# Layernorm on ScalarE, later transposes, and earlier loads in a fused attention and ReGLU kernel on one core

## The chip, the core and the metric

The kernel runs on one core of one Trainium2 chip. The core has a matrix engine (TensorE, PE in the profile, with its weight loads listed apart as PEld), VectorE (DVE), ScalarE (ACT), GpSimd (POOL), and SyncE (SP), which here only issues DMA transfers. Each engine works through its own instructions in order and waits on semaphores for the others. The metric is the device time of one execution in microseconds, as the median of several runs.

## The reference

`x` has 2048 rows (tokens) of 576 columns, float32.

```python
xn = layernorm(x)                                  # over the 576 columns, eps 1e-5
q, k, v = split(xn @ wqkv)                         # 32 heads of 18 columns
s = softmax(q @ k.T * 18**-0.5) @ v @ wo           # full attention, per head
gate = xn @ W_gate; gate = gate * (gate > 0)       # 576 -> 4608
B = (gate * (xn @ W_up)) @ W_down                  # 4608 -> 576
return x + s * silu(B)
```

## The kernel before

Every float32 operand of a matmul is split into a high and a low part in the matmul's reduced format, and each product is made of three matmuls (high x high, high x low, low x high). `split_full` does this for results in PSUM: ScalarE copies the high part out, VectorE subtracts for the low part. `split_pool` does it for weights: POOL casts, then subtracts.

Matmuls use 64 of the 128 rows of the array, and two of them run at the same time on the two halves: two *lanes*. A planner, the class `Lanes`, writes PE's order out by hand (`keep` fixes program order). `lanes.window(parts, scores, inserts)` issues the parts of the two lanes in turn; `inserts` are calls that are made when a given share of the window has been issued. When a lane must start a bank that the other lane ended, `part` puts a fence on ScalarE or VectorE, and the matmul waits for it.

The first stage goes through four groups `g` of 512 tokens. The rows of group 0 are loaded, their statistics taken (`stats`: bn_stats and bn_aggr on VectorE, then a square root on ScalarE and a refined reciprocal), normalized (`normalized_rows`, into `xn`, with 64 extra columns that repeat the last ones), and turned (`turn`: four PE transposes per chunk of 128 columns into `tps`, five chunks, split into the tile `x`). Then, for each group, one window holds the q and k products (`pq`: four pairs of head blocks with the weights `wqk0` to `wqk3`, and at odd groups `qk_last` with `wqk4`), 216 matmuls of 512 columns, 270 at odd groups. In this window the next group is normalized and turned, by inserts from `rows_to_features`. A second window holds 216 matmuls for v (`pv`, weights `wv`). q, k and v go out to DRAM (`qd`, `kd`, `vd`).

In the last group, the memory of the transposed rows `xB` is given to a pool `at` of key and query tiles (`kT`, `qT`), filled by many small loads on SP (`load_k`, `load_q`); score maxima (`pm`) of the first heads run between the v products.

The long loop follows: `cycle(k)` computes two units of 128 hidden columns each, gate and up products (`pg`, `pu`, with the split weights `gw` of `up_weights`), their product `hh`, the down product (`py`, weights `dw`), and between them the attention of two heads. In `cycle(0)` the order of the two units on the two lanes is "+U +W -U -W". A tail applies `wo` and the last sum.

Of the kernel before, what the change touches and what calls it, by code (L numbers as in the profile page):

```python
# [9 lines left out]
F32 = mybir.dt.float32  # L10
# [18 lines left out]
class Lanes:  # L29
# [4 lines left out]
    def __init__(self, banks, make, matmul, fence):  # L34
        self.make, self.matmul, self.fence = make, matmul, fence
        self.t = [0.0, 0.0]
        self.last = 0.0
        self.free = [0.0] * banks
        self.used = [False] * banks
        self.server = {"V": 0.0, "A": 0.0}  # L40
        self.main = [deque(), deque()]
        self.n = self.synced = self.fences = 0
        self.wrote = [0] * banks
        self.left = []

    def take(self, now):
# [84 lines left out]
        return p.open + self.FENCE <= self.t[lane]  # L131

    def part(self, p):
        by = min("AV", key=lambda e: self.server[e])
        self.fence(by, p.ps)
        self.fences += 1
        p.open = max(self.server[by], p.end + self.FENCE)
        self.server[by] = p.open
# [69 lines left out]
def kernel(  # L208
# [46 lines left out]
    def keep(ins):  # L255
        return tc.keep_in_program_order(ins)
# [37 lines left out]
    def split_pool(hi, lo, raw):  # L294
        keep(nc.gpsimd.tensor_copy(hi, raw))  # L295
        keep(nc.gpsimd.tensor_tensor(lo, raw, hi.bitcast(F32), ALU.subtract))  # L296
# [113 lines left out]
    with ExitStack() as st:  # L410
# [1 line left out]
        xBs = st.enter_context(ExitStack())  # L412
        xB = pool(xBs, "xB", KX + 1, "right")

        def weights(name, n, outs, pl=one, first=False, **kw):
            gw = pl.tile([P, 2, KS, n], F32R, name=name, **kw)
            o = 0
            for cols in outs:
                m = sum(c[2] for c in cols[0])
                rg = one.tile([P, KS, P], F32, tag="rgw", name="rgw", bufs=2)[:, :, :m]  # L420
                load9(rg, cols)
                hi, lo = gw[:, 0, :, o : o + m], gw[:, 1, :, o : o + m]
                if first:
                    nc.scalar.activation(hi, rg, AF.Copy)
                    nc.gpsimd.tensor_tensor(lo, rg, hi.bitcast(F32), ALU.subtract)
                else:
                    split_pool(hi, lo, rg)
                o += m
            return gw

        def load_rows(g):
            xt = one.tile([P, 4, D], F32, name="xt", bufs=2)
            if g == 0:
                for j in range(4):
                    nc.sync.dma_start(xt[:, j], x2[j * P : (j + 1) * P, :])
            else:
                nc.sync.dma_start(xt, rows512(x2, g))
            return xt

        def stats(xt, ln):  # L440

            stat = one.tile([P, 4, 2, 6], F32, name="stat")
            mv = one.tile([P, 4, 2], F32, name="mv")
            for j in range(4):
                for h in range(2):
                    keep(nc.vector.bn_stats(stat[:, j, h, :], xt[:, j, h * HC : (h + 1) * HC]))
                keep(nc.vector.bn_aggr(mv[:, j, :], stat[:, j, :, :]))
                yield
            ve, sd, r0, r1, r2, rs = (
                one.tile([P, 4], F32, name=f"ln{i}") for i in range(6)  # L450
            )
            keep(nc.vector.tensor_scalar(ve, mv[:, :, 1], EPS, None, op0=ALU.add))
            nc.scalar.activation(sd, ve, AF.Sqrt)
            nc.vector.reciprocal(r0, sd)
            nc.vector.tensor_tensor(r1, r0, r0, ALU.mult)
            nc.vector.tensor_tensor(r2, r1, ve, ALU.mult)
            nc.vector.tensor_scalar(r1, r2, -0.5, 1.5, op0=ALU.mult, op1=ALU.add)
            nc.vector.tensor_tensor(rs, r0, r1, ALU.mult)
            ln += [xt, mv, rs]
            yield  # L460

        def normalized_rows(xt, mv, rs, xn):
            for j in range(4):
                nc.vector.tensor_scalar(
                    xn[:, j, :D], xt[:, j], mv[:, j, 0:1], rs[:, j : j + 1], op0=ALU.subtract, op1=ALU.mult
                )
                nc.vector.tensor_scalar(
                    xn[:, j, D:], xt[:, j, C4:], mv[:, j, 0:1], rs[:, j : j + 1], op0=ALU.subtract, op1=ALU.mult
                )
                if j % 2:  # L470
                    yield

        def turn(g, xn, i):

# [49 lines left out]
        def qk_last(gw, g):  # L524
            return pair(
                ("pq", "pq"), (xs[g], xs[g + 1]), lambda rows, s, a, xr: (gw[rows, a, s, :], xr),
                512, [qk_steps(4, g + m, m, True) for m in range(2)],
            )
# [37 lines left out]
        wqk = []  # L566

        def qk_weights(b):
            kw = dict(pl=ws, tag="gw") if b == 3 else {}
            wqk.append(  # L570
                weights(f"wqk{b}", P, [[[(wqkv, b * P, P)], [(wqkv, D + b * P, P)]]], first=b < 2, **kw)
            )

        qk_weights(0)
        qk_weights(1)
        nxt = load_rows(1)
        qk_weights(2)
        qk_weights(3)
        wv = weights(
            "wv", HC, [[[(wqkv, 2 * D + m * VH, VH)], [(wqkv, 2 * D + HC + m * VH, VH)]] for m in range(3)]  # L580
        )
        wqk.append(weights("wqk4", P, [[[(wqkv, C4, DT), (wqkv, D + C4, DT)]] * 2], pl=ws, tag="gw"))
        xn0 = one.tile([P, 4, D + DT], F32, name="xn")
        for _ in normalized_rows(*ln0, xn0):
            pass
        for i in range(KX):
            turn(0, xn0, i)

        def stepped(gen, at_):
            return [(w, lambda: next(gen, None)) for w in at_]  # L590

        for g in range(NQ):
            fill = iter(())
            if g + 1 < NQ:
                fill = rows_to_features(g + 1, nxt)
            pairs = [qk_pair(b, wqk[b], g) for b in range(4)]
            first = pairs[:2] + ([qk_last(wqk[4], g - 1)] if g % 2 else [])
            parts = [a + b for a, b in zip(in_turn(first), in_turn(pairs[2:]))]
            spread = [0.1 + 0.85 * i / 12 for i in range(12)]
            ins = stepped(fill, spread)  # L600
            lanes.window(parts, None, ins)
            if g + 1 < NQ:
                spill(g)
            if g + 2 < NQ:
                nxt = load_rows(g + 2)
            if g == NQ - 1:
                xBs.close()
                at = pool(right, "at", 1, "right")
                for i in range(NRING):
                    kT = at.tile([P, 512], F32R, name=f"kT{i}")  # L610
                    nc.gpsimd.memset(kT.bitcast(F32), 1.0)
                    ring.append(kT)
                load_q(0, 0)
                for c in range(NQ):
                    load_k(0, c)
                load_q(0, 1)
                up_weights(0)
                pms = [maxima(0, h) for h in range(2)]
            vp = v_pairs(wv, g)
            va_, vb_ = in_turn(vp[:2]), in_turn(vp[2:])  # L620
            scores = None
            if g == NQ - 1:
                scores = [(deque(pms[h].popleft() for _ in range(NP)), deque()) for h in range(2)]
            lanes.window([a + b for a, b in zip(va_, vb_)], scores)
            for _ in fill:
                pass

    two = pool(right, "two", 2, "right")
    acc = right.enter_context(ExitStack())
# [241 lines left out]
    def cycle(k, scores):  # L871

        up_weights(k + 1)
        ups = []
        ins = []
        downs = down(k - 1) if k else []
        down_weights(k)
        sums = dict(zip("UWabcd", [up(k), up(k + 1), *downs]))
        if k > N1:
            orders = ("+a +U -a +b -U +W -b +c -W +d -c -d", "+a +U -a -U +b +W -b +c -W +d -c -d")  # L880
        elif k:
            orders = ("+U +a -U +b -a -b +W +c -W +d -c -d",) * 2
        else:
            orders = ("+U +W -U -W",) * 2
        parts = [[sums[o[1]][l ^ (o[0] == "-")] for o in orders[l].split()] for l in range(2)]
        turn_over = units[k + 1][1] == NF - 1 and k + 2 < len(units)
        ins.append((0.55, lambda: (gus.pop(k), up_weights(k + 2))))

        if turn_over:
            ins.append((0.8, lambda: load_x(units[k + 2][0], 0)))  # L890
        lanes.window(parts, scores, ins)
        gus.pop(k + 1)
        down_weights(k + 1)
        if k:
            store_y(k - 1)
        if turn_over:
            del xcur[units[k][0]]
            for c in range(1, KX):
                load_x(units[k + 2][0], c)
# [180 lines left out]
```

## Time and profile before

| | us |
|---|---|
| median of 3 runs | 2640.25 (2640.12 to 2640.27) |
| profiled execution | 2642.54 |
| its span | 2640.5 |
| PE busy in it | 2607.2 |
| DVE, ACT, POOL busy | 1733.0, 1464.0, 1442.1 |
| mean granted TensorE clock | 0.996 |

The profile records one execution. Its span runs from the first to the last recorded instruction; 2.04 us lie around it. In rows of the timeline the first number is the start in us from the beginning of the span, the second the duration, then engine, line, operation, output and inputs with their shapes, the count, and in brackets how long the engine had been idle and what released it. Rows of groups give busy time and the mean of one instruction in ns. A matmul's duration overlaps with the next ones', so the pace of a run of matmuls is read from their starts.

### The profile page before, as it was taken

The page shows a single profiled execution, that of the slowest core. Times are in us where ns is not written, and L with a number is a line of the kernel's source. Part 1 is how long each engine was busy: PE and PEld are TensorE (multiplying, and loading weights), DVE is VectorE, ACT ScalarE, POOL GpSimd, SP SyncE. Part 2 cuts the span into 40 slices and gives each one's busy share as a digit, 9 for nine tenths or more (in the row PEclk, how much of TensorE's full clock was granted, in tenths as well). Part 3 has the DMA queues.
Part 4 walks back from the last instruction along what each step waited for, and adds up shares of the span by engine and source line. Part 5 has one row for each costly group of instructions (what it writes and reads, how often), then busy time and mean ns, then how long its engine had stood idle before and what let it go on. Part 6 is the DMA issues. An engine that isn't in the chain of part 4 may idle for free.

```text
span 2640.5 us, 62759 instructions
## 1 busy us (share of the span) xinstructions
PE 2607.2 (99%) x25436; PEld 2119.1 (80%) x25436; DVE 1733.0 (66%) x2888; ACT 1464.0 (55%) x2755; POOL 1442.1 (55%) x1273
## 2 busy tenths in 40 slices
PE   7998999999999999999999999999999999999999
PEld 5997887778887777777778778887777777778789
DVE  5325557777777777777777777777777777776124
ACT  2221226666666666666666666666666666666662
POOL 5234886555555555555555555555555555555555
PEclk9998999999999999999999999999999999999999
DMA  8644332222232222222242222222233222222247
GB/s 253 201 145 147 88 87 74 71 69 72 83 115 72 67 70 73 74 73 74 69 132 63 67 75 66 75 71 72 73 99 89 70 76 70 74 66 56 59 123 237
DMA packets 293265, 243.69 MB, mean 92 GB/s; under 512 B 64496, under 2 KB 236272, under 8 KB 292976
## 3 DMA queue, kind: packets, MB, share of 16 engines
q1 hardware_dynamic: 286192, 216.08, 28.2%
q0 software_dynamic: 6784, 23.60, 2.8%
q8 instruction: 201, 3.29, 0.5%
q14 instruction: 88, 0.72, 0.1%
HBM read 193.45 MB, written 45.61 MB: 91 GB/s over the span
## 4 chain that ended last, share of the span: by engine, by line
PE 93%; DMA 2%; POOL 2%; SPq 1%; DVE 1%; ACT 0%; issue 0%; POOLq 0%; ACTq 0%; DVEq 0%
PE pg L259 22%; PE po L259 17%; PE py L259 16%; PE pu L259 11%; PE pm L259 9%; PE psx L259 9%; PE pq L259 4%; PE pv L259 2%; PE pw L259 1%; PE tp L262 1%; SPq L353 1%; PE tps L262 1%; DMA rg<-in_B_W_up_dram 1%; DMA kT<-kd 1%; DMA gt<-yd 0%; DMA out_dram<-xr 0%
## 5 line engine op out<-in xcount | busy, mean ns | idle before, releaser
L383 DVE TENSOR_REDUCE mx<-pm 128x1 f32<-128x512 f32 x2048 | 1379.1, 689 | 254.4 <-PE pm L259 168.5
L817 ACT ACTIVATE p<-psx 128x512 f32<-128x512 f32 x2048 | 1182.3, 598 | 542.1 <-PE psx L259 258.8
L259 PE MATMUL pg<-x,gw 64*128 64x512 f32 x3888 | 1159.7, 392 | 5.7 <-POOL gw L296 3.7
L259 PE MATMUL pu<-x,gw 64*128 64x512 f32 x3888 | 1146.9, 392 | 0.0
L259 PE MATMUL pm<-kT,qT 54*128 54x512 f32 x2048 | 794.1, 398 | 3.0 <-DMA kT<-kd 3.0
L259 PE MATMUL psx<-qT,kT 56*128 56x512 f32 x2048 | 786.3, 394 | 0.0
L259 PEld LDWEIGHTS pg<-x,gw 64*128 64x128 f32 x3888 | 721.0, 187 | 60.5 <-POOL gw L296 4.6
L259 PEld LDWEIGHTS pu<-x,gw 64*128 64x128 f32 x3888 | 718.9, 187 | 25.0
L259 PE MATMUL py<-dw,hh 64*128 64x288 f32 x6864 | 717.5, 295 | 1.4 <-POOL dw L296 0.3
L259 PEld LDWEIGHTS py<-dw,hh 64*128 64x128 f32 x6864 | 662.8, 186 | 49.3 <-issue 30.1
L259 PE MATMUL po<-p,va 128*32 128x512 f32 x4096 | 452.7, 594 | 0.4 <-ACT p L817 0.4
L667 POOL CAST hh<-h 128x512 fp32r<-128x512 f32 x127 | 77.6, 611 | 612.3 <-DVE h L664 612.3
L694 POOL TENSOR_TENSOR y<-yt,y 128x288 f32<-128x288 f32 x268 | 215.2, 806 | 323.7 <-ACT yt L693 323.5
L259 PEld LDWEIGHTS psx<-qT,kT 56*128 56x128 f32 x2048 | 375.3, 185 | 18.9
L296 POOL TENSOR_TENSOR gw<-rg,gw 128x1152 fp32r<-128x1152 f32 x144 | 383.5, 2664 | 11.6
L259 PEld LDWEIGHTS pm<-kT,qT 54*128 54x128 f32 x2048 | 372.4, 185 | 18.5 <-issue 3.2
L259 PEld LDWEIGHTS po<-p,va 128*32 128x32 f32 x4096 | 126.4, 110 | 279.1 <-issue 269.1
L296 POOL TENSOR_TENSOR dw<-rd,dw 128x576 fp32r<-128x576 f32 x144 | 204.9, 1423 | 11.5
L670 POOL TENSOR_TENSOR hh<-h,hh 128x512 fp32r<-128x512 f32 x144 | 186.3, 1294 | 38.0 <-ACT hh L669 27.8
L295 POOL CAST gw<-rg 128x1152 fp32r<-128x1152 f32 x144 | 165.2, 1147 | 18.0 <-DMA rg<-in_B_W_up_dram 11.5
L689 DVE TENSOR_TENSOR y<-py,y 128x288 f32<-128x288 f32 x268 | 120.2, 449 | 49.5 <-PE py L259 48.9
L660 ACT ACTIVATE h<-pg 128x512 f32<-128x512 f32 x144 | 85.9, 597 | 116.7 <-PE pg L259 56.2
(80 smaller groups left out, 1353.0 us busy)
## 6 DMA issues: line engine op xcount, KB each, us to landing
rd<-in_B_W_down_dram SPq DMA_DIRECT2D x144, 288.0 KB
rg<-in_B_W_gate_dram SPq DMA_DIRECT2D x144, 256.0 KB
rg<-in_B_W_up_dram SPq DMA_DIRECT2D x144, 256.0 KB
qT<-qd SPq DMA_DIRECT2D x384, 36.0 KB
kT<-kd SPq DMA_DIRECT2D x384, 36.0 KB
kd<-hh POOLq DMA_DIRECT2D x16, 512.0 KB, 4.6
qd<-hh POOLq DMA_DIRECT2D x16, 512.0 KB, 5.7
xTd<-x SPq DMA_DIRECT2D x15, 512.0 KB
```

What stands on the lines that cost most here:

```text
L259: return keep(nc.tensor.matmul(*args, **kw))
L262: return keep(nc.tensor.transpose(*args))
L295: keep(nc.gpsimd.tensor_copy(hi, raw))
L296: keep(nc.gpsimd.tensor_tensor(lo, raw, hi.bitcast(F32), ALU.subtract))
L353: nc.sync.dma_start(dst[r0 : r0 + DH, :].bitcast(F32), src[i, f0 : f0 + DH, cs])
L383: nc.vector.tensor_reduce(mx[:, g % 2, h, j, c : c + 1], ps, axis=AX.X, op=ALU.max)
L660: nc.scalar.activation(made[0], ps, AF.Relu)
L667: keep(nc.gpsimd.tensor_copy(hh[:, 0], h))
L670: keep(nc.gpsimd.tensor_tensor(hh[:, 1], h, hh[:, 0].bitcast(F32), ALU.subtract))
L689: nc.vector.tensor_tensor(ys[j][:, cs], ps[:, :HC], ys[j][:, cs], ALU.add)
L694: keep(nc.gpsimd.tensor_tensor(ys[j][:, cs], t, ys[j][:, cs], ALU.add))
L817: nc.scalar.activation(p[0][:, h, i, :], ps, AF.Exp, scale=SCALE)
```

## The change

Seven edits, most of them in the first stage:

- Normalized rows are made by ScalarE (Identity with a scale and a bias per row) in place of VectorE's two-operand operation; the extra columns are one ScalarE copy. The small layernorm operations move from VectorE to POOL, and the square root takes eps as its bias.
- `wqk0` and `wqk1` are cast by POOL, no longer by ScalarE. `wqk3` has a buffer of its own.
- The rows of group 1 are loaded ahead of the second weight block. `wv` and `wqk4` are loaded and split in the first window, at 0.12 of it.
- Of group 0 only the first chunk is turned ahead of the products; the others are inserted three matmuls ahead of their first use. In later groups statistics, normalizing and turning stand at other shares of the window.
- The window of the last group is cut in two. After its first part the pool `at` is opened, the weights of unit 0 are asked for, and keys and queries are loaded; after its second part the weights of unit 1.
- In the first stage fences go to ScalarE only (`by`).
- `cycle(0)` has the order "+U -U +W -W".

```diff
     def part(self, p):
-        by = min("AV", key=lambda e: self.server[e])
+        by = min(self.by, key=lambda e: self.server[e])
...
-                if first:
-                    nc.scalar.activation(hi, rg, AF.Copy)
-                    nc.gpsimd.tensor_tensor(lo, rg, hi.bitcast(F32), ALU.subtract)
-                else:
-                    split_pool(hi, lo, rg)
+                split_pool(hi, lo, rg)
...
-            keep(nc.vector.tensor_scalar(ve, mv[:, :, 1], EPS, None, op0=ALU.add))
-            nc.scalar.activation(sd, ve, AF.Sqrt)
+            nc.scalar.activation(sd, mv[:, :, 1], AF.Sqrt, bias=eps[:, 0:1])
             nc.vector.reciprocal(r0, sd)
-            nc.vector.tensor_tensor(r1, r0, r0, ALU.mult)
-            nc.vector.tensor_tensor(r2, r1, ve, ALU.mult)
-            nc.vector.tensor_scalar(r1, r2, -0.5, 1.5, op0=ALU.mult, op1=ALU.add)
-            nc.vector.tensor_tensor(rs, r0, r1, ALU.mult)
+            for fn in (
+                lambda: nc.gpsimd.tensor_tensor(ve, mv[:, :, 1], eps, ALU.add),
+                lambda: nc.gpsimd.tensor_scalar(nm, mv[:, :, 0], -1.0, None, op0=ALU.mult),
+                lambda: nc.gpsimd.tensor_tensor(r1, r0, r0, ALU.mult),
+                lambda: nc.gpsimd.tensor_tensor(r2, r1, ve, ALU.mult),
+                lambda: nc.gpsimd.tensor_scalar(r1, r2, -0.5, 1.5, op0=ALU.mult, op1=ALU.add),
+                lambda: nc.gpsimd.tensor_tensor(rs, r0, r1, ALU.mult),
+                lambda: nc.gpsimd.tensor_tensor(nb, nm, rs, ALU.mult),
+            ):
+                keep(fn())
...
-                nc.vector.tensor_scalar(
-                    xn[:, j, :D], xt[:, j], mv[:, j, 0:1], rs[:, j : j + 1], op0=ALU.subtract, op1=ALU.mult
-                )
-                nc.vector.tensor_scalar(
-                    xn[:, j, D:], xt[:, j, C4:], mv[:, j, 0:1], rs[:, j : j + 1], op0=ALU.subtract, op1=ALU.mult
-                )
+                nc.scalar.activation(
+                    xn[:, j, :D], xt[:, j], AF.Identity, bias=nb[:, j : j + 1], scale=rs[:, j : j + 1]
+                )
                 if j % 2:
                     yield
+            nc.scalar.activation(xn[:, :, D:], xn[:, :, C4:D], AF.Copy)
...
         qk_weights(0)
+        nxt = load_rows(1)
         qk_weights(1)
-        nxt = load_rows(1)
         qk_weights(2)
         qk_weights(3)
...
-        for i in range(KX):
-            turn(0, xn0, i)
+        turn(0, xn0, 0)
...
+        spread = [0.05, 0.06, 0.07, 0.08, 0.09, 0.3, 0.35, *(0.55 + 0.09 * i for i in range(KX))]
         for g in range(NQ):
...
-            spread = [0.1 + 0.85 * i / 12 for i in range(12)]
             ins = stepped(fill, spread)
-            lanes.window(parts, None, ins)
+            if g == 0:
+                first = in_turn(pairs[:2])
+                ins.append((0.12, late_weights))
+                ins += [((6 * i - 3) / 216, lambda i=i: turn(0, xn0, i)) for i in range(1, KX)]
...
+            if g < NQ - 1:
+                lanes.window([a + b for a, b in zip(first, second)], None, ins)
+            else:
+                lanes.window(first)
                 xBs.close()
                 at = pool(right, "at", 1, "right")
+                up_weights(0)
...
                 load_q(0, 1)
-                up_weights(0)
+                lanes.window(second)
+                up_weights(1)
...
-            orders = ("+U +W -U -W",) * 2
+            orders = ("+U -U +W -W",) * 2
```

More of the change, by code (lines that the diff above doesn't have):

```diff
@@ L43, in __init__ @@
         self.wrote = [0] * banks
+        self.by = "A"
         self.left = []
@@ L413, with weights @@
         xB = pool(xBs, "xB", KX + 1, "right")
-        def weights(name, n, outs, pl=one, first=False, **kw):
+        def weights(name, n, outs, pl=one, **kw):
             gw = pl.tile([P, 2, KS, n], F32R, name=name, **kw)
@@ L438, in load_rows @@
             return xt
+        eps = one.tile([P, 4], F32, name="eps")
+        nc.gpsimd.memset(eps, EPS)
         def stats(xt, ln):
@@ L448, in stats, with normalized_rows @@
                 yield
-            ve, sd, r0, r1, r2, rs = (
-                one.tile([P, 4], F32, name=f"ln{i}") for i in range(6)
-            )
-            keep(nc.vector.tensor_scalar(ve, mv[:, :, 1], EPS, None, op0=ALU.add))
-            nc.scalar.activation(sd, ve, AF.Sqrt)
+            ve, sd, r0, r1, r2, rs, nm, nb = (
+                one.tile([P, 4], F32, name=f"ln{i}") for i in range(8)
+            )
+            nc.scalar.activation(sd, mv[:, :, 1], AF.Sqrt, bias=eps[:, 0:1])
             nc.vector.reciprocal(r0, sd)
-            nc.vector.tensor_tensor(r1, r0, r0, ALU.mult)
-            nc.vector.tensor_tensor(r2, r1, ve, ALU.mult)
-            nc.vector.tensor_scalar(r1, r2, -0.5, 1.5, op0=ALU.mult, op1=ALU.add)
-            nc.vector.tensor_tensor(rs, r0, r1, ALU.mult)
-            ln += [xt, mv, rs]
+            for fn in (
[8 more added lines that the diff above has]
+                keep(fn())
+            ln += [xt, rs, nb]
             yield
-        def normalized_rows(xt, mv, rs, xn):
+        def normalized_rows(xt, rs, nb, xn):
             for j in range(4):
-                nc.vector.tensor_scalar(
-                    xn[:, j, :D], xt[:, j], mv[:, j, 0:1], rs[:, j : j + 1], op0=ALU.subtract, op1=ALU.mult
-                )
-                nc.vector.tensor_scalar(
-                    xn[:, j, D:], xt[:, j, C4:], mv[:, j, 0:1], rs[:, j : j + 1], op0=ALU.subtract, op1=ALU.mult
+                nc.scalar.activation(
+                    xn[:, j, :D], xt[:, j], AF.Identity, bias=nb[:, j : j + 1], scale=rs[:, j : j + 1]
                 )
@@ L568, in qk_weights, with late_weights @@
         def qk_weights(b):
-            kw = dict(pl=ws, tag="gw") if b == 3 else {}
-            wqk.append(
-                weights(f"wqk{b}", P, [[[(wqkv, b * P, P)], [(wqkv, D + b * P, P)]]], first=b < 2, **kw)
-            )
+            wqk.append(weights(f"wqk{b}", P, [[[(wqkv, b * P, P)], [(wqkv, D + b * P, P)]]]))
         qk_weights(0)
+        nxt = load_rows(1)
         qk_weights(1)
-        nxt = load_rows(1)
         qk_weights(2)
         qk_weights(3)
[L579 to L582, printed above, removed]
+        wvs = []
+        def late_weights():
+            outs = [[[(wqkv, 2 * D + m * VH, VH)], [(wqkv, 2 * D + HC + m * VH, VH)]] for m in range(3)]
+            wvs.append(weights("wv", HC, outs))
+            wqk.append(weights("wqk4", P, [[[(wqkv, C4, DT), (wqkv, D + C4, DT)]] * 2], pl=ws, tag="gw"))
         xn0 = one.tile([P, 4, D + DT], F32, name="xn")
@@ L596 @@
             pairs = [qk_pair(b, wqk[b], g) for b in range(4)]
-            first = pairs[:2] + ([qk_last(wqk[4], g - 1)] if g % 2 else [])
-            parts = [a + b for a, b in zip(in_turn(first), in_turn(pairs[2:]))]
-            spread = [0.1 + 0.85 * i / 12 for i in range(12)]
             ins = stepped(fill, spread)
-            lanes.window(parts, None, ins)
[L602 to L606, printed above, removed]
+            if g == 0:
+                first = in_turn(pairs[:2])
+                ins.append((0.12, late_weights))
+                ins += [((6 * i - 3) / 216, lambda i=i: turn(0, xn0, i)) for i in range(1, KX)]
+            elif g == 2:
+                first = in_turn(pairs[:2])
+            else:
+                first = in_turn([*pairs[:2], qk_last(wqk[4], g - 1)])
+            second = in_turn(pairs[2:])
+            if g < NQ - 1:
+                lanes.window([a + b for a, b in zip(first, second)], None, ins)
+            else:
+                lanes.window(first)
                 xBs.close()
                 at = pool(right, "at", 1, "right")
+                up_weights(0)
                 for i in range(NRING):
@@ L616 @@
                 load_q(0, 1)
-                up_weights(0)
+                lanes.window(second)
+                up_weights(1)
                 pms = [maxima(0, h) for h in range(2)]
-            vp = v_pairs(wv, g)
+            if g + 1 < NQ:
+                spill(g)
+            if g + 2 < NQ:
+                nxt = load_rows(g + 2)
+            vp = v_pairs(wvs[0], g)
             va_, vb_ = in_turn(vp[:2]), in_turn(vp[2:])
@@ L626 @@
                 pass
+        lanes.by = "AV"
     two = pool(right, "two", 2, "right")
```

## The prediction

> **What bounds the kernel now.** I read the busy shares on the page first, then the table of windows, then the timeline wherever the windows show TensorE (PE) short of full. The first fence is the page's line of busy times and four windows: length, PE busy with its matmul count, weight loads, DVE, ACT, POOL, granted clock, DMA share, GB/s.
>
> ```profile
> PE 2607.2 (99%) x25436; PEld 2119.1 (80%) x25436; DVE 1733.0 (66%) x2888; ACT 1464.0 (55%) x2755; POOL 1442.1 (55%) x1273
> ...
> 0.00:20.00 20.00, 4.25 (x17) 3.40 (x18) 13.96 (x29) 5.61 (x7) 9.19 (x16) 1.00 0.81 236
> 20.00:40.00 20.00, 17.80 (x137) 13.61 (x135) 13.72 (x30) 3.46 (x7) 16.52 (x11) 0.97 0.53 140
> 60.00:200.00 140.00, 140.00 (x1441) 130.14 (x1441) 41.44 (x92) 30.81 (x64) 40.52 (x56) 1.00 0.56 181
> 240.00:260.00 20.00, 18.26 (x156) 15.37 (x156) 7.70 (x13) 2.54 (x6) 11.60 (x10) 0.82 0.39 112
> ```
>
> PE works 99% of the span, and the change neither adds nor removes a matmul. So only PE's idle time, and time at a lowered clock, can be won. From 60 to 200 us PE is full: moving normalization there from VectorE to ScalarE is worth nothing, because the other engines have slack (DVE 41 of 140 us, ACT 31) and PE does not. After 260 us the built order of the changed kernel is the old one apart from a few swaps. What is left is two places: the start (0 to 57 us) and the entry into the long loop (200 to 260 us).
>
> **The start before.** Timeline rows (start, duration, engine, line, operation, idle before and releaser):
>
> ```profile
> 8.03 0.21 DVE L447 BATCH_NORM_AGGREGATE mv<-stat 128x2 f32<-128x12 f32 x1
> 8.48 0.20 ACT L453 ACTIVATE ln<-ln 128x4 f32<-128x4 f32 x1 [6.46 <-DVE ln L452]
> 10.93 2.62 DVE L467 TENSOR_SCALAR xn<-xt,mv,ln 128x64 f32<-128x64 f32 x1
> 13.46 2.91 DVE L464 TENSOR_SCALAR xn<-xt,mv,ln 128x576 f32<-128x576 f32 x1
> 10.73 5.32 POOL L425 TENSOR_TENSOR wqk<-rgw,wqk 128x1152 fp32r<-128x1152 f32 x2 [7.67 <-ACT wqk L424]
> 17.15 3.89 PE L262 MATMUL tps<-ident,xn 128*128 128x128 f32 x17 [0.24 <-DVE xn L464]
> 20.97 15.79 PE L259 MATMUL pq<-x,wqk 64*128 64x512 f32 x129
> 38.35 0.30 PE L262 MATMUL tps<-ident,xn 128*128 128x128 f32 x1 [1.59 <-DVE xn L464]
> 40.86 3.78 PE L259 MATMUL pq<-x,wqk 64*128 64x512 f32 x15
> 56.97 3.28 PE L259 MATMUL pv<-wv,x 64*128 64x288 f32 x44
> ```
>
> Two VectorE normalizations last 2.62 and 2.91 us beside POOL's subtraction; so transposes start late and the first product is at 20.97. A second hole runs from 36.76 to 40.86, again for normalized rows. The v products begin at 57.0.
>
> **The start after.** Prices:
>
> ```profile
> 2556.10 1.28 ACT L1005 ACTIVATE wo<-rw 128x576 fp32r<-128x576 f32 x2 [0.42 <-DMA rw<-in_A_wo_dram]
> 2564.42 1.28 ACT L970 ACT_TABLE_LOAD   x1 [5.80 <-DMA gt<-yd]
> 2565.71 1.48 ACT L970 ACTIVATE sg<-gt 128x576 f32<-128x576 f32 x2
> 17.66 0.60 ACT L290 ACTIVATE x<-tps 128x512 fp32r<-128x512 f32 x1 [5.03 <-PE tps L262]
> 18.29 0.69 DVE L291 TENSOR_TENSOR x<-tps,x 128x512 fp32r<-128x512 f32 x1 [0.97 <-ACT x L290]
> 47.69 0.66 PE L262 MATMUL tps<-ident,xn 128*128 128x128 f32 x4
> 166.12 20.22 PE L259 MATMUL pq<-x,wqk 64*128 64x512 f32 x172
> L296 POOL TENSOR_TENSOR gw<-rg,gw 128x1152 fp32r<-128x1152 f32 x144 | 383.5, 2664 | 11.6
> L295 POOL CAST gw<-rg 128x1152 fp32r<-128x1152 f32 x144 | 165.2, 1147 | 18.0 <-DMA rg<-in_B_W_up_dram 11.5
> L694 POOL TENSOR_TENSOR y<-yt,y 128x288 f32<-128x288 f32 x268 | 215.2, 806 | 323.7 <-ACT yt L693 323.5
> ```
>
> First product. Statistics are done at 8.24 as before. In the changed order ScalarE's wait for them stands ahead of the table load, which used to run at once: 1.28, as in the row at 2564.42 after its own wait, to 9.55. Square root 0.20, reciprocal, to about 9.97. Then five dependent POOL operations on 4 columns. No such row exists; POOL's subtractions of 1152 and 288 columns (2.66 and 0.81) extrapolate to 0.19 at none, and with a hand-over I take 0.27 (from 0.19 to 0.40): 1.35, to 11.35. Four activations of 576 columns at 0.60 (1.28 less 0.68 for the second of two), to 13.8, and the copy of the extra columns to 14.2. Four transposes, ScalarE's copy: the first product at about 14.9, six us earlier than 20.97. (By the rows at 2564.42 and 2565.71 the activation follows the load by 0.01. The Trainium skill, "ScalarE: Activation LUTs", What ACT_TABLE_LOAD costs, adds a drain of about 1.38 us to the load's 1.28; I can't see it in this trace. By that rule the first product comes at 16.3 and the gain below is at most 1.4 us smaller.)
>
> What the six us are worth. The products that follow need chunks 1 to 4, and each is now turned behind only three products of the one before: 0.66 for transposes, 0.60 for ScalarE, 0.69 for VectorE, and hand-overs, about 2.1 us a chunk. Before, the chunks followed each other at 0.85 (17 in 3.89). So from 14.3, five chunks end near 24.8, with some 27 of the 216 products done; products cost (20.22 - 0.39) / 171 = 0.116 each.
>
> Next, the second lane's next bank may be written only once a fence has passed, and all fences of this stage now stand in ScalarE's queue. The 80th matmul (20 transposes, 60 products) waits for a fence that is queued behind the first activation of the next group's normalization. That needs POOL's seven small operations, which stand in POOL's queue behind the splits of four weight blocks, two of which ScalarE used to cast: four times 1.15 + 2.66, from some 11.4, with 1.8 of waiting for the second block (3.54 MB lie ahead of its end: at 236 GB/s, from about 2, it lands at 17.0 and not 15.2), then 1.9 of small operations and 0.7 of ScalarE: free at about 31.0. PE is there at 24.8 + 33 x 0.116 = 28.6: a new stall of 2.4. Then 156 products (18.1) and five turns of the next group at 0.9 each, their rows ready by then, so the hole of 36.76 to 40.86 is gone: v starts at 53.6, a gain of 3.4.
>
> That is at full clock. In 14.3 to 24.8 PE is busy for some 1.0 of each 2.1 us. If that lowers the clock, a chunk takes 2.67, the fifth ends at 27.6, and products cost twice as much until a full interval has passed (about 32.0): 21 in that time, then 168 x 0.116 + 4.5, and v starts at 56.0: a gain of 1.0, with the fence no longer in the way. I take the middle, **2.2 us**, both ends kept. (The window 0 to 20 shows clock 1.00 with 4.25 us of work in 20, and the products from 20.97 run at full pitch at once. The Trainium skill, "TensorE: Matmul & The Clock Gate", Part 1, has PE cold after an idle window of about 3.4 us and warm after one of steady work: this trace disagrees at the start and agrees later, where the clock falls behind holes. By it the end of 1.0 is the right one.)
>
> The v weights, now split late, take POOL three times at most 3.81 from 31: done by 43, read at 53.6. Later groups' statistics and rows keep margins of that kind. I cost both at nothing; were the cover gone, PE would wait the difference.
>
> **The entry to the loop.** Rows of PE, POOL and SP:
>
> ```profile
> 205.90 0.58 PE L259 MATMUL pm<-kT,qT 54*128 54x512 f32 x1 [2.96 <-DMA kT<-kd]
> 235.64 0.49 PE L259 MATMUL pg<-x,gw 64*128 64x512 f32 x1 [2.03 <-POOL gw L295]
> 238.34 0.79 PE L259 MATMUL pg<-x,gw 64*128 64x512 f32 x1 [1.96 <-POOL gw L296]
> 253.34 0.50 PE L259 MATMUL pg<-x,gw 64*128 64x512 f32 x1 [1.74 <-POOL gw L296]
> 254.35 0.62 PE L259 MATMUL pg<-x,gw 64*128 64x512 f32 x1
> 254.77 0.62 PE L259 MATMUL pg<-x,gw 64*128 64x512 f32 x1
> 257.33 0.39 PE L259 MATMUL pg<-x,gw 64*128 64x512 f32 x1
> 257.56 0.39 PE L259 MATMUL pg<-x,gw 64*128 64x512 f32 x1
> 238.24 2.51 POOL L670 TENSOR_TENSOR hh<-h,hh 128x512 fp32r<-128x512 f32 x2
> 249.43 1.15 POOL L295 CAST gw<-rg 128x1152 fp32r<-128x1152 f32 x1 [6.58 <-PE py L259]
> 238.91 4.56 SPq L353 DMA_DIRECT2D qT<-qd  x11
> 243.57 0.41 SPq L339 DMA_DIRECT2D rg<-in_B_W_gate_dram  x1
> ```
>
> Behind each stall pairs of products come every 0.42 us (254.35, 254.77) and not every 0.23 (257.33, 257.56), until 257.3 in the last case, some 3.4 us. That half-clock stretch costs 3.4 x (1 - 0.23/0.42) = 1.5 to 1.6.
>
> Keys: their tiles lie where the old transposed rows lay. In both built orders SP's first load of them waits for the same product, the last one that reads that memory, number 1580 of PE's matmuls, and the loads behind it keep their order. So cutting the last window in two brings them no earlier against PE: the 2.96 at 205.90 stays. I cost this at 0; the rival below has the other price.
>
> Third weight block (the stalls at 235.64 and 238.34): with "+U -U +W -W" the first product of gate and up is ready sooner, and its subtraction (half of 2.51, 1.27) now stands in POOL's queue ahead of this split. It ends 1.3 later; most of that falls in half-clock time, so it costs 0.7 (to 1.3).
>
> Fourth weight block (253.34): its load on SP comes five issues earlier, 5 x 4.56 / 11 = 2.1: at 241.5. Load and split then take what they took, 249.43 + 1.22 + 2.66 - 243.57 = 9.7, to 251.2. PE needs it at 253.34 - 1.74 = 251.6, now 0.7 later, 252.3. So the stall and its half-clock stretch go: +3.3 (if it is only shortened, +1). Switching lanes in the new cycle order may wait for an eviction, up to 0.7, taken at 0.4. Sum **+2.2 us** (0.5 to 3.3).
>
> **The sum.** 2.2 + 2.2 = 4.4. The profiled execution took 2642.54 (span 2640.5 and 2.04 around it); 2642.54 - 4.4 = 2638.1. The median of the runs is 2640.25, 2.3 lower, so the forecast is 2635.8, with its own ends 2633.5 (3.4 + 3.3) and 2638.7 (1.0 + 0.5).
>
> **Rivals.**
>
> The start is as good as it looks: no serial chunks, no fence, no second hole. 14.9 + 216 x 0.116 + 9 turns of 0.9 = 48.1, against 57.0: 8.9, with 2.2 gives 2629.1. For it: the products do start six us earlier. Against it: the order of chunks leaves nothing to do between them. 16 in 100.
>
> The keys do come earlier: 2.96 and its slow stretch of 1.6 go as well: 2635.8 - 4.5 = 2631.3. For it: half the window stands between. Against it: the same product releases the first load. 10 in 100.
>
> Little remains: the start runs at low clock (+1.0), and the fourth block still stalls while the third is later (-0.7 and -0.4): 2640.4. For it: the half-busy start, and the margin of 1 us on the fourth block. 18 in 100.
>
> Slower: the fence on ScalarE is released late because POOL's queue is held by strips that land late; the next rows' 1.18 MB go ahead of the second strip. If the queue moves 140 GB/s (window 20 to 40) and not 236 (0 to 20), the second strip lands at 3.54 / 0.140 + 2 = 27.3, the three splits from there end at 38.7, and the fence passes at 41.3. Then v starts at 41.3 + 22.6 + 1.6 for the clock = 65.5, 8.5 late; with +2.2 that is 6.3 us slower: 2646.5. It decides once the fence passes after about 35. For it: the queue is the only supply, and five things hang on it in series. Against it: the first 20 us did move 236. 13 in 100.
>
> **The numbers.** The forecast has the other 43 in 100. The 0.2% that a measurement of this kernel can tell is 5.3 us, below 2635.0 or above 2645.5. Faster: the first two rivals (26) and 13 of the forecast's 43 (2633.5 to 2635.0 of its 2633.5 to 2638.7). Slower: the last rival, 13. Within: 30 of the forecast and 18 of the third rival, 48. Range 2629.0 to 2641.0: it leaves out the slower case and a little below.
>
> **What would show it.** First product near 15 (16.3 with a drain); then groups of four transposes 2.1 apart; a PE wait near 28 to 31 released through ScalarE; no hole for normalized rows after that; v from 53.6 to 56.0. The kT stall of about 3 us still there, some 20 us behind the first load; the split of the third block behind a subtraction of 1.27; no stall for the fourth. From there both traces should run parallel. I am wrong if the first turn's chunks overlap, if the fence is not what PE waits for, if the key stall goes, or if the traces part after 260 us.

## The result, and the profile after

The changed kernel is slower: 2646.62 us median of 10 runs beside 2640.59 of 10 of the kernel before, ratio 1.0024 (95% interval 1.0014 to 1.0033). Single runs of these two kernels lie up to 4 us from their median, so places and causes are read from the traces, and ratios stand beside them. Its profiled execution took 2646.69 us, span 2644.8: 4.3 more than before, where the medians differ by 6.0 (the profiled execution of the kernel before lay 2 above its median). By PE's own milestones:

| us | before | after | difference |
|---|---|---|---|
| first q/k product | 20.97 | 15.78 | -5.2 |
| v products of group 0 begin | 56.97 | 57.41 | +0.4 |
| wait for the fourth key tile ends | 205.90 | 210.80 | +4.9 |
| second wait for the third weight block ends | 238.34 | 245.19 | +6.9 |
| first wait for an eviction behind the fourth weight block ends | 263.75 | 267.43 | +3.7 |
| end | 2640.5 | 2644.8 | +4.3 |

The five us at the front are gone before v begins; 4.5 are lost in or just behind the first v window; two more at the entry to the loop, where 3.2 come back with the fourth block. Another 0.6 is lost behind that, which no run looks into. Windows of the profile after (columns as in the prediction), and all waits of PE that are over 1 us:

```profile
0.00:20.00 20.00, 6.12 (x17) 2.90 (x17) 5.54 (x15) 6.33 (x9) 9.59 (x19) 1.00 0.74 226
20.00:40.00 20.00, 20.00 (x110) 13.32 (x110) 6.97 (x18) 6.75 (x11) 15.56 (x16) 1.00 0.52 138
60.00:200.00 140.00, 136.72 (x1393) 121.81 (x1391) 31.63 (x63) 36.87 (x73) 41.32 (x66) 0.99 0.56 184
240.00:260.00 20.00, 15.54 (x130) 13.53 (x132) 7.64 (x12) 3.23 (x8) 15.42 (x12) 0.83 0.48 140
```
```profile
PE tps L263 <- ACT xn L469: 13.1, 4, 12.2
PE pv L260 <- ACTq L282: 3.3, 1, 3.3
PE pm L260 <- DMA kT<-kd: 3.2, 1, 3.2
PE pg L260 <- POOL gw L296: 3.1, 1, 3.1
PE pg L260 <- POOL gw L297: 2.0, 1, 2.0
```

From 20 to 40 us PE counts as busy throughout, with 110 matmuls, where before it was busy for 17.8 us with 137. That is not full work. PE runs at half pace there until about 32 us, as shown below. And while the chunks come in, up to 27.9 us, products also wait for the split of their chunk, which only the rows of the weight loads (PEld) show:

```profile
18.93 0.29 PEld L260 LDWEIGHTS pq<-x,wqk 64*128 64x128 f32 x2 [0.47 <-ACT x L291]
19.66 0.29 PEld L260 LDWEIGHTS pq<-x,wqk 64*128 64x128 f32 x2 [0.44 <-DVE x L292]
```

And 60 to 200, full before, now has a hole. It is the second line of waits: a v product waits for ScalarE's sequencer at the line of the fences. The timeline around it, and the window of the three us that follow:

```profile
61.39 0.60 ACT L291 ACTIVATE hh<-pq 128x512 fp32r<-128x512 f32 x1 [1.45 <-DMA qd<-hh]
62.02 0.69 DVE L292 TENSOR_TENSOR hh<-pq,hh 128x512 fp32r<-128x512 f32 x1 [1.35 <-ACT hh L291]
66.32 0.21 DVE L447 BATCH_NORM_AGGREGATE mv<-stat 128x2 f32<-128x12 f32 x1
66.57 0.30 ACT L452 ACTIVATE ln<-mv,eps 128x4 f32<-128x4 f32 x1 [4.58 <-DVE mv L447]
66.76 5.49 PE L260 MATMUL pv<-wv,x 64*128 64x288 f32 x58 [3.27 <-ACTq L282]
```
```profile
67.00:70.00 3.00, 3.00 (x28) 3.00 (x30) 0.14 (x1) 0.64 (x2) 0.00 (x0) 0.52 1.06 358
```

The square root of group 2's statistics stands in ScalarE's order ahead of the second pair of fences of this window. It waits for the last aggregate on VectorE, which came to the statistics only after the last q/k eviction at 62.02; ScalarE's part of that eviction, at 61.39, had waited for an earlier store of queries. PE goes on when the square root has been issued, and runs at a granted clock of 0.52 for the next three us.

### The profile page after: what moved, and what is told of

It reads as the page before. It is cut to its first block, busy times and chain, and to the rows that moved or that the text cites. A ratio compares the mean times of both kernels' runs of the same rounds, so it can differ in the third digit from the quotient of the medians.

```text
span 2644.8 us, 62737 instructions
## 1 busy us (share of the span) xinstructions
PE 2612.3 (99%) x25436; PEld 2119.8 (80%) x25436; DVE 1709.8 (65%) x2836; ACT 1476.2 (56%) x2773; POOL 1449.6 (55%) x1304
## 4 chain that ended last, share of the span: by engine, by line
PE 94%; DMA 2%; POOL 2%; DVE 1%; ACT 1%; SPq 1%; issue 0%; POOLq 0%; ACTq 0%; DVEq 0%
PE pg L260 22%; PE po L260 17%; PE py L260 16%; PE pu L260 12%; PE pm L260 10%; PE psx L260 9%; PE pq L260 3%; PE pv L260 2%; PE pw L260 1%; PE tp L263 1%; PE tps L263 1%; DMA qd<-hh 0%; DMA out_dram<-xr 0%; DMA gt<-yd 0%; DMA kT<-kd 0%
```

## The experiments

**Both fence engines.** One edit to the changed kernel:

```diff
-        self.by = "A"
+        self.by = "AV"
```

> The changed kernel with fences of the first stage on ScalarE or VectorE again, as before the change; all else as changed. Theory 1 (a fence in the first v window stood in ScalarE's queue behind the square root of a later group's statistics, which waits for VectorE): the 3.27 us PE wait at 66.76 and the half-clock stretch behind it (about 1.5) go; the products for v start at 57.4 as in the changed kernel; profiled span 2644.8 - 4.8 = 2640.0, median about 5 us below the changed kernel. Rival (what is late is VectorE's own work, held up by transfers of keys and queries, so a fence on VectorE is late as well): a wait of about 3 us stays, span 2644 to 2645.

```profile
57.85 14.44 PE L260 MATMUL pv<-wv,x 64*128 64x288 f32 x207
```

Span 2639.2, ratio to the kernel before 0.9999 (0.9990 to 1.0008). The v window runs through in 14.44 us; the wait and the slow stretch are gone, 5.6 us against an expected 4.8. Theory 1 holds: the wait came from a fence behind the square root. With this one edit undone the ratio shows neither a loss nor a gain. Two other single edits below (one piece, more buffers) bring the ratio to 1.000 as well.

**A busy TensorE ahead of the start.** Before `turn(0, xn0, 0)`, with 44 and then 76 repetitions:

```diff
+        for _ in range(44):
+            tp(ps[:, :P], ident, ident)
```

> As the run with both fence engines, and in addition 44 transposes of the identity on TensorE ahead of the first real transpose, while it would be idle; their result is not used. Theory (the start is slow because PE is at half clock while its work comes in trickles): the chunks of group 0 follow each other at 2.2 to 2.4 us and not 3.25, v starts at 53 to 54 and not 57.4, span about 3.5 below the run with both fence engines, 2636.5. Rival (the chunk pace is set by hand-overs between engines, not by the clock): the pace stays near 3.2, v starts at 57, span as in the run with both fence engines.

With 44 the row of unused transposes ended at 8.25, and the first real one came at 12.59, so PE was idle for 4.3 us; chunks stayed 3.25 apart, v began at 57.69, span 2639.2, ratio 1.0003 (0.9994 to 1.0012). Inconclusive, since PE was cold again behind the gap (granted clock 0.50 from 13 to 16 us). Hence the second:

> As the run with 44 unused transposes and both fence engines, but with 76, so that TensorE is busy until the first real transpose and no idle stretch of 4 us lies between. Theory (half clock in the trickling start costs what was expected of it): chunks of group 0 follow each other at 2.2 to 2.5 us, not 3.25, v starts at 53 to 54.5 and not 57.85, span about 2636. Rival (a start that is half busy falls to half clock by itself within some 3 to 7 us, however warm it began): only the first one or two chunks are fast, v starts at 56 or later, span above 2638.

```profile
14.39 0.33 PE L263 MATMUL tps<-ident,xn 128*128 128x128 f32 x1 [0.43 <-ACT xn L469]
15.50 1.42 PE L260 MATMUL pq<-x,wqk 64*128 64x512 f32 x3 [0.78 <-ACT x L291]
16.85 1.11 PE L263 MATMUL tps<-ident,xn 128*128 128x128 f32 x4
17.89 2.28 PE L260 MATMUL pq<-x,wqk 64*128 64x512 f32 x6
20.10 1.11 PE L263 MATMUL tps<-ident,xn 128*128 128x128 f32 x4
```

The first four transposes take 0.33 each (0.47 to 0.48 in the kernel after), so PE is warm. But they come 0.76 apart, one per activation of 576 columns, and by the first products the half pace is back: four transposes in 1.11 us where 0.66 is full pace, chunks 3.25 apart. v began at 56.96. The rival holds: a trickling start falls to half clock by itself, and here the record of the clock says so too (the 0.50, granted clock):

```profile
15.00:18.00 3.00, 2.50 (x9) 1.42 (x9) 0.69 (x1) 0.35 (x2) 2.00 (x2) 0.50 0.49 116
```

No run has the trickle at full clock, so how much of the 3.25 us is the clock and how much the waits for the split stays open. (The span of 2644.9 here, ratio 1.0017 (1.0008 to 1.0026), has another wait in it, 3.75 us in the v window for a fence on VectorE.)

**The last group's window in one piece.**

```diff
-                lanes.window(first)
+                lanes.window([a + b for a, b in zip(first, second)])
...
-                up_weights(0)          # ahead of the key loads
-                lanes.window(second)
-                up_weights(1)
+                up_weights(0)          # behind them
```

> The changed kernel with the last group's window in one piece again, and key loads and the first weight block asked for behind it, as before the change. Theory (the same product releases the key loads in both): first key load, PE's wait for the fourth key tile (3.2 us) and the span stay within 0.5 us of the changed kernel's, 2644.3 to 2645.3. Rival (the cut does bring keys earlier): the wait for keys grows by 1 us or more, span above 2646.

```profile
210.66 0.76 PE L260 MATMUL pm<-kT,qT 54*128 54x512 f32 x1 [3.31 <-DMA kT<-kd]
239.43 0.50 PE L260 MATMUL pg<-x,gw 64*128 64x512 f32 x1 [0.86 <-POOL gw L296]
227.99 0.36 SPq L655 DMA_DIRECT2D rd<-in_B_W_down_dram  x1
238.23 1.14 POOL L296 CAST gw<-rg 128x1152 fp32r<-128x1152 f32 x1 [3.06 <-DMA rg<-in_B_W_up_dram]
```

and the same steps of the kernel after:

```profile
210.80 0.76 PE L260 MATMUL pm<-kT,qT 54*128 54x512 f32 x1 [3.21 <-DMA kT<-kd]
242.48 0.49 PE L260 MATMUL pg<-x,gw 64*128 64x512 f32 x1 [3.06 <-POOL gw L296]
234.80 0.36 SPq L657 DMA_DIRECT2D rd<-in_B_W_down_dram  x1
237.96 0.66 POOL L296 CAST dw<-rd 128x576 fp32r<-128x576 f32 x1 [8.80 <-DMA rd<-in_B_W_down_dram]
240.07 1.27 POOL L684 TENSOR_TENSOR hh<-h,hh 128x512 fp32r<-128x512 f32 x1
241.29 1.14 POOL L296 CAST gw<-rg 128x1152 fp32r<-128x1152 f32 x1
```

Keys come at the same time and with the same wait, as the first load's wait in both built orders had it. But the span is 2642.3, 2.5 lower, which neither theory had. By the ratio, 1.0003 (0.9994 to 1.0012) against 1.0024, it is some 5 us; the profiled execution was the slowest of its ten. The cut does move something: with it the load of the third gate and up block goes out at 218.88, ahead of key loads on SP, and the first down load (`rd`) at 234.80 instead of 227.99. POOL takes that down block before the third gate and up block, so the third is split at 241.29 instead of 238.23, and PE's first wait for it is 3.06 instead of 0.86. (This wait began at 239.42 with the cut and at 238.57 without; where the 0.9 ahead of it comes from is not shown.)

The kernel before has the same order as the kernel after, though its window is whole:

```profile
214.14 0.39 SPq L339 DMA_DIRECT2D rg<-in_B_W_gate_dram  x1
229.07 0.36 SPq L643 DMA_DIRECT2D rd<-in_B_W_down_dram  x1
232.35 0.67 POOL L295 CAST dw<-rd 128x576 fp32r<-128x576 f32 x1 [10.45 <-DMA rd<-in_B_W_down_dram]
234.44 1.14 POOL L295 CAST gw<-rg 128x1152 fp32r<-128x1152 f32 x1
```

So the one-piece run does not bring the old order back. It has a third one, in which the third block is asked for at 233.32, behind the first down load. In the changed kernel the cut costs 2.5 us or more against a whole window; that it made this order worse than in the kernel before is not shown.

**The old order of the first cycle.**

```diff
-            orders = ("+U -U +W -W",) * 2
+            orders = ("+U +W -U -W",) * 2
```

> The changed kernel with the old order +U +W -U -W in the first cycle. Theory: the third weight block is split about 1 us earlier (PE's wait of 3.06 falls to about 2), but the wait for the fourth (1.7) and its half-clock stretch (1.6) come back: span 2644.8 - 0.9 + 3.3 = 2647. Rival (the fourth block's gain comes from elsewhere, loads asked for earlier): no wait for the fourth block, span about 2644.

```profile
241.30 0.49 PE L260 MATMUL pg<-x,gw 64*128 64x512 f32 x1 [3.79 <-POOL gw L296]
...
259.49 0.79 PE L260 MATMUL pg<-x,gw 64*128 64x512 f32 x1 [1.96 <-POOL gw L297]
```

Span 2647.0, as expected, and the wait for the fourth block is back at 259.49. The third block is split 1.2 earlier, as the theory had it (240.11 and not 241.29); PE's wait for it is longer (3.79 against 3.06) because PE came to it sooner still. The traces end 2.2 us apart. But where the second wait for the third block ends, the run with the old order was 1.2 ahead (244.00 against 245.19), so the fourth block costs it 3.4 in the trace. The ratio, 1.0025 (1.0014 to 1.0035), doesn't separate the two orders (1.0024 for the changed kernel).

**All five chunks turned first** (with both fence engines):

```diff
-        turn(0, xn0, 0)
+        for i in range(KX):
+            turn(0, xn0, i)
```

> The run with both fence engines, with all five chunks of group 0 turned ahead of the first product, as before the change. Theory: chunks follow each other at about 0.9, the first product comes near 18.5 and five chunks are done there and not at 28; PE is at full clock from about 23; then PE waits some 5 to 8 us near 25 to 33 for a fence that stands behind the next group's normalization in ScalarE's queue, and falls to half clock: v starts at 56 to 58, span 2638 to 2640. Rival (that fence is not what PE waits for): no wait, v starts at 52 or earlier, span about 2634.

```profile
14.46 3.89 PE L263 MATMUL tps<-ident,xn 128*128 128x128 f32 x17 [0.28 <-ACT xn L469]
18.27 10.40 PE L260 MATMUL pq<-x,wqk 64*128 64x512 f32 x85
32.74 5.53 PE L260 MATMUL pq<-x,wqk 64*128 64x512 f32 x34 [4.07 <-ACTq L282]
60.49 10.74 PE L260 MATMUL pv<-wv,x 64*128 64x288 f32 x156 [2.41 <-DVEq L282]
```

The predicted fence is real: PE stops for 4.07 us until 32.74, behind ScalarE's normalizing. v still begins at 53.7, 4.1 earlier than with trickling chunks, better than the 56 to 58 expected. Then a new wait of 2.41 stands in the v window, for a fence on VectorE. Span 2637.6, but the profiled execution was among the fastest (2639.66 beside a median of 2643.08), and the ratio of 1.0002 (0.9993 to 1.0012) doesn't show the gain.

**Sums of these.** One-piece window with both fence engines:

> Both fence engines in the first stage and the last group's window in one piece, the rest as changed. Theory (the two faults add up: 5.6 for the fences, 2.5 for the later load of the first down weights): span 2644.8 - 8.1 = 2636.7, faster than the kernel before by 3 to 4 us. Rival (the shorter wait in the one-piece run came from the shift of times behind the fence): span as with both fence engines alone, 2639.

Span 2636.0, ratio 0.9979 (0.9969 to 0.9988): the two faults add up, and without them the rest of the change is worth some 5 us. Then with chunks first, and every fence of the stage on VectorE (`self.by = "V"`):

> One-piece window, all five chunks turned first, and all fences of the first stage on VectorE, which has little left to do there. Theory: no fence waits for ScalarE's normalization; PE waits at most 3 us for one behind the next group's statistics; v starts at 52 to 55, span 2632 to 2636. Rival (PE gets to the v products sooner, and then waits for key and query stores, which hold evictions and the fences behind them): a wait of 2 us or more in the v window, span 2636 or more.

```profile
57.97 0.60 ACT L291 ACTIVATE hh<-pq 128x512 fp32r<-128x512 f32 x1 [7.47 <-DMA kd<-hh]
47.84 4.38 PE L260 MATMUL pv<-wv,x 64*128 64x288 f32 x57
61.29 10.99 PE L260 MATMUL pv<-wv,x 64*128 64x288 f32 x132 [9.07 <-DVEq L282]
```

Span 2635.8, ratio 0.9984 (0.9975 to 0.9993), no better than the run before it. v begins at 47.84, nine us earlier than before, and PE then waits 9.07 until 61.29. The rival holds: ScalarE's copy of keys waited 7.47 for an earlier store from the same buffer.

**More buffers for split keys and queries.** In `qk_steps`:

```diff
-                    made.append(hp.tile([P, 2, 512], F32R, name="hh", bufs=4))
+                    own = b == 2 or (b == 3 and m == 0)
+                    made.append(
+                        one.tile([P, 2, 512], F32R, tag="qk", name="hh", bufs=3) if own
+                        else hp.tile([P, 2, 512], F32R, name="hh", bufs=4)
+                    )
```

> One-piece window, five chunks first and fences on VectorE as in the run that waited 9.07 us in the first v window, and in addition three more buffers for the split keys and queries of a group (the third pair and half of the fourth), so that seven of the eight evictions of a group need no earlier store to have landed. Theory (that wait comes from evictions that wait for the stores of keys and queries to DRAM on a full DMA queue): the wait falls from 9.07 to 2 or less, the second half-clock stretch goes, span 2626 to 2630. Rival (the fence is late for another reason, or the last eviction still waits as long): a wait of 6 us or more, span 2633 to 2636.

```profile
48.56 14.44 PE L260 MATMUL pv<-wv,x 64*128 64x288 f32 x210
```

Span 2623.9, median 2626.06, ratio 0.9944 (0.9931 to 0.9958). No wait is left in the first stage between the first product and the keys. This version beats both kernels. And the same buffers alone in the changed kernel:

> The changed kernel with only these three more buffers; fences still on ScalarE alone, the square root still ahead of the second pair of them. Theory (the square root is late because VectorE reaches the statistics only after evictions that waited for stores): the wait of 3.27 in the first v window falls below 1, span 2639.5 to 2641. Rival (the rows of the later group land late, and the statistics wait for them): the wait stays at 2 us or more, span 2643 or more.

```profile
62.94 0.30 ACT L452 ACTIVATE ln<-mv,eps 128x4 f32<-128x4 f32 x1 [4.58 <-DVE mv L447]
```

The square root comes at 62.94 and not 66.57, and PE no longer waits in the v window, though the fences still stand behind it. PE's first wait for the third gate and up block grows to 6.66 us, and the span is 2638.1 (ratio 1.0001, 0.9992 to 1.0010). So the chain is stores, evictions, statistics, square root, fence, PE; taking away either end is enough here. (With both fence engines a fence on VectorE was late instead in two other runs, by 3.75 and 2.41 us.)

**Two edits to the fastest version.** A square root of a constant at the start, to load the table early:

> The kernel with the one-piece window, chunks first, fences on VectorE and three more buffers, and in addition one square root of a constant on ScalarE at the very start, its result unused, so that the function table is loaded before the statistics are there. Theory (the load of 1.28 us stands on the path to the first transpose): first transpose 1.0 to 1.3 earlier, span 1 to 1.3 lower, 2622.6 to 2623. Rival (the reciprocal and POOL's small operations wait for something else): first transpose and span as without it, 2623.9.

The table load is back at 0.74, the first transpose at 11.09 instead of 12.52, v at 47.60 instead of 48.56: theory confirmed there. But the span is 2626.4: a wait of 2.5 us for the third weight block has come up, which the base version didn't have. Ratio 0.9942 (0.9927 to 0.9957); not to be told from the base version's. And normalizing on VectorE again:

> The same base kernel with layernorm's small operations and the normalizing on VectorE, as before the change; weight splits all on POOL as changed. Theory (beside POOL's subtractions VectorE's normalizing takes up to 2.9 us an instruction and not 0.57, so moving it to ScalarE was worth some us): first four transposes done 2 us or more later, or a hole for normalized rows of group 1, span 2626 to 2630. Rival (the move is worth nothing): span within 1 us of 2623.9.

```profile
10.20 2.96 DVE L464 TENSOR_SCALAR xn<-xt,mv,ln 128x576 f32<-128x576 f32 x1
28.80 1.85 DVE L458 TENSOR_TENSOR ln<-ln,ln 128x4 f32<-128x4 f32 x1
30.76 9.28 PE L260 MATMUL pq<-x,wqk 64*128 64x512 f32 x59 [4.78 <-DVEq L282]
```

Span 2632.1, 8.2 more; ratio 0.9966 (0.9952 to 0.9980). The instruction beside POOL's subtraction takes 2.96 us again, yet the first product comes at 18.69, as early as without this edit (18.62): the later start of the theory did not come. The time goes behind it. PE waits 4.78 us for a fence on VectorE, which stands behind layernorm's small operations; two of these took 2.15 and 1.85 us beside POOL's subtractions, where the first of them took 0.16 for group 0. So moving this work off VectorE was a good edit where the fences stand on VectorE. What it is worth with fences elsewhere was not run.

## Why the prediction was wrong

The forecast was a gain of 4.4 us, to 2635.8; the median came out at 2646.62. By the milestones, up to v the change gave -0.4 where +2.2 was forecast, from there to the keys -4.5 where nothing was, at the entry to the loop +1.2 where +2.2 was, and -0.6 came behind it.

The step that failed first is the sentence on the later groups, that "later groups' statistics and rows keep margins of that kind", and with it the terms for stage one behind 57 us, costed at nothing. I had weighed the fence queue only in the first q/k window. The same queue holds a worse case in the first v window: the square root of group 2 moved ahead of fences there. Price: 3.27 and a slow stretch, 5.6 us by the run that undoes it. My rival for "slower" had the right mechanism, a fence on ScalarE behind something late, at the wrong place and through the wrong supply: strips of weights did not land late (the third q/k block waited 1.09 for its load), stores of keys and queries did. That its time, 2646.5, is near the measured one is luck.

The start: the chain to the first product was nearly right (14.9 forecast, 15.78 measured):

```profile
8.08 1.28 ACT L452 ACT_TABLE_LOAD   x1 [8.08 <-DVE mv L447]
9.38 0.30 ACT L452 ACTIVATE ln<-mv,eps 128x4 f32<-128x4 f32 x1
11.33 3.14 ACT L469 ACTIVATE xn<-xt,ln,ln 128x576 f32<-128x576 f32 x4 [1.65 <-POOL ln L461]
```

The table load stands where forecast. The activation follows it by 0.02, so no drain of 1.38 shows behind it. The four activations took 3.14 and not 2.4: I took the price of a plain copy, and these read a scale and a bias per row. (The Trainium skill, "ScalarE: Activation LUTs", What ACT_TABLE_LOAD costs, has about 0.28 us + 0.833 ns a column with one such operand, 0.09 more for a second and 0.09 of overlap. By its figures that is an estimate of 0.76 each at 576 columns; transposes one activation apart began 0.76 apart, 12.25 and 13.01.)

The value of that lead was the end I named for half clock, and worse: chunks came every 3.25 us, where I had 2.67, and v at 57.4, where I had 56.0; the middle I took was no measurement. My 2.67 left a piece out: behind the subtraction of a chunk stand two more of its products, and the next transposes come only behind these (weight loads at 19.66, next transposes at 20.39): 0.73 a chunk. The fence I had near 28 to 31 us held nothing up, as that low end had it; it shows when the chunks are turned first (the 4.07 above). I had let the clock column decide against a cold start. Matmuls per window decide otherwise. Before, and then after:

```profile
20.00:23.00 3.00, 3.00 (x19) 2.35 (x19) 2.68 (x5) 1.19 (x2) 3.00 (x2) 1.00 0.45 175
23.00:26.00 3.00, 3.00 (x28) 2.42 (x28) 1.05 (x4) 0.00 (x0) 2.92 (x2) 1.00 0.61 148
```
```profile
29.00:32.00 3.00, 3.00 (x14) 2.12 (x14) 0.66 (x3) 0.77 (x2) 1.88 (x8) 1.00 0.61 142
32.00:35.00 3.00, 3.00 (x26) 2.49 (x26) 0.00 (x0) 2.97 (x5) 2.92 (x3) 1.00 0.03 5
```

The kernel before warms up by 23 us and the one after by about 32, and the column reads 1.00 in all four rows. (So the rule of the Trainium skill that I set aside, in "TensorE: Matmul & The Clock Gate", Part 1, holds here: cold after idleness, warm after a steady stretch.) The 0.85 a chunk that I read off the kernel before was a half-pace price too: its 17 transposes took 3.89 us, and at the pace of four in 0.66, one in 0.33, I estimate 2.1.

The entry to the loop: keys no earlier, right. The fourth block's stall gone, right; the new cycle order did it, and 3.2 came back there where I had 3.3. The third block later, right in sign, but by 2.0 and not 0.7: the subtraction of 1.27 ahead of it cost its whole time, and the down block ahead of both was split 5.6 later than before (237.96, 232.35) with PE 4.9 late; why is not shown. The cut of the window, costed at 0, is the second step that failed: in the changed kernel it costs 2.5 us in the traces, some 5 by the ratios. So this part gave 1.2 and not 2.2: the lag of 4.9 at the key wait is 3.7 behind the fourth block.

## What to carry to other kernels

When fences or evictions are put on one in-order engine, list everything else in that engine's built order up to each fence, and what each of those waits for, over the whole stage; one tiny operation with a late input is enough. Before a start is made earlier, find what its far end waits for: here stores held the buffers, and 9 us won at the front were 9 us of waiting until three more buffers were there. Work fed to TensorE in trickles can cost more than starting later in one piece: here v began 4.1 us earlier with all chunks turned first.

## What the hardware showed that was not expected

At the start the granted clock reads 1.00 while matmuls run at half pace: four transposes in 1.11 us against 0.66, and 14 matmuls in 3 us against 26. Once PE had been warm, in the run with 76 unused transposes, half pace reads 0.50. Count matmuls in a window rather than read the clock, at the start above all. And 76 unused transposes up to 11.3 us did not keep PE warm through four transposes at 0.76 spacing.
